# Linear attention and a mixture of four experts: k's last 64 rows multiplied as 64 partitions instead of zero-padded 128

## The chip, the core and the metric

The kernel runs on one core of a Trainium2 chip. The metric is the device time of one execution in microseconds (us), lower is better. The engines are named as the profile names them: PE is TensorE's matmul and PEld its weight load, DVE is VectorE, ACT is ScalarE, POOL is GpSimd and SP is SyncE, which only issues transfers here.

## What is computed

The reference is linear attention followed by four experts whose outputs are merged by the given probabilities:

```python
phi(x) = where(x > 0, x, exp(x) - 1) + 1        # q, k, v: (8, 8, 576, 64)
kv  = einsum('bhsd,bhse->bhde', phi(k), v)
z   = sum(phi(k), axis=2)
num = einsum('bhsd,bhde->bhse', phi(q), kv)
den = einsum('bhsd,bhd->bhs', phi(q), z) + 1e-6
x   = (num / den), as (4608, 512)
out = sum over e of p[:, e] * (relu(x @ w1[e]) @ w2[e])   # w1: (4, 512, 1024)
```

There are 8 batches of 8 heads, 576 rows to a head and 64 numbers to a row. The sum over the 576 rows in `kv` is where the change lies.

## The kernel before, in words

A head's 576 rows are four chunks of 128 and a rest of 64. The chunks go through the batch one after the other; the rests are kept apart. One tile, `rl`, holds the rests of k, v and q of a batch: partitions 0 to 63 have the 64 rest rows of heads 0 to 3, partitions 64 to 127 those of heads 4 to 7 (`load_left`, line 248).

**Phi.** It is computed as min(exp(x), max(x + 1, 1)) and written as f16. For the chunks `phi_act` and `phi_dve` (lines 303 and 318) write it. For the rests `left_act` and `left_dve` (lines 337 and 363) do. In batches 1 to 7 ScalarE writes x + 1 (line 351) and the exponential (line 355), the latter to PSUM, and VectorE joins them in one operation (line 367). In batch 0 ScalarE writes the exponential alone, and VectorE does two operations (lines 371 and 372). For q's rests each of these is one operation over 128 partitions. For k's rests the exponential is one operation, and each of the others is two, of 64 partitions, for they go to different columns of a tile with zeros: `kz` is 128 partitions x 4 pairs of heads x 128, and each pair has its phi in only one half of the partitions (the upper for heads 0 to 3, the lower for 4 to 7). The rest stays at the zero that line 134 writes once, at the start.

**Products of k and v.** `kv` (line 418) makes, for a pair of heads, one accumulation of five matmuls with 130 columns: four for the chunks (line 425) and one for the rest (line 432). Of the latter `kz[:, pair]` is the stationary operand with all 128 partitions, and the moving operand is `vl[:, 2a : 2a+2]`, which has the rests of v of two pairs, one in each half of the partitions. The zeros of `kz` take the wrong half out. The columns are 64 numbers for each of two heads, and for each a constant column that gives z. ScalarE then copies the two useful blocks to `kvz` (line 441). With 8 batches and 4 pairs there are 32 matmuls on line 432, between 128 on line 425. Numerators and denominators follow from `kvz` (`nd`, line 455; `nd_left`, line 478), and then x transposed.

**Experts.** Each of 9 token tiles (one of each batch, and one of all the rests) goes through the 4 experts. Layer 1 is made of seven products of half-size blocks, layer 2 of seven more (lines 730 and 668), with block sums of the hidden values on POOL (lines 635 to 641), relu on ACT and DVE (lines 714, 756 and 774) and the weighted sum of the outputs on DVE (line 570). The first tile with the first expert is done plainly (lines 524 and 579).

**Order.** The order of every engine's queue is written out by hand: a schedule is held fixed for PE, ACT, DVE, SP and POOL. Batch 0 follows the list `START`, in which a number stands for so many warming matmuls on a tile of zeros (line 857); `lka` and `lkd` are the phi of k's rests. The rest is a list of steps with positions that is sorted (`put_at`, line 919, and `work.sort`, line 992); `batch_steps` (line 799) places batch b + 1's attention among the experts of tile b, by the positions in `ATTN`. There `lk`, `lkd` and `kv` place ScalarE's part of k's rests, VectorE's part, and the products. The positions are the same before and after.

Weights come in through POOL's queue and most inputs through SP's. For batch 0, k's rests are the first transfer on SP.

Of the kernel before, what the change touches and what calls it, by code (L numbers as in the profile page):

```python
# [11 lines left out]
FP16 = mybir.dt.float16  # L12
# [18 lines left out]
            k=(-2.05, 25.8, 28.0, 28.5),  # L31
# [19 lines left out]
            k=(0.3, 2.9, 6.7, 11.25),  # L51
# [29 lines left out]
def kernel(  # L81
# [10 lines left out]
    nc = tc.nc  # L92
    ATTN, HSUM, L2ORD, L2AT, MODE = (CFG[x] for x in ("ATTN", "HSUM", "L2ORD", "L2AT", "MODE"))

    B, H, S, D = q.shape
# [3 lines left out]
    P = 128  # L99
    HP = P // 2  # L100
# [4 lines left out]
    HG = H // 2  # L105
    NPAIR = H // 2
# [17 lines left out]
    pconst = ctx.enter_context(tc.tile_pool(name="pconst", bufs=1))  # L124
# [5 lines left out]
    nc.gpsimd.memset(vl[:, :, D:DE], 1.0 / SX)  # L130
    qz = pconst.tile([P, 2, 2, P], FP16, tag="qz", name="qz")
    nc.vector.memset(qz, 0.0)
    kz = pconst.tile([P, NPAIR, P], FP16, tag="kz", name="kz")
    nc.vector.memset(kz, 0.0)
    kvzs = []
    for i in range(2):
        kvz = pconst.tile([P, NPAIR, 2, DE], FP16, tag=f"kvz{i}", name=f"kvz{i}")
# [31 lines left out]
    def aps(shape, dtype, name):  # L169
        return bank("aps", shape, dtype, name)  # L170
# [67 lines left out]
    class Batch:  # L238
        def __init__(self, b):
            self.b = b  # L240
            self.raw, self.ph, self.pairs = {}, {}, {}
            self.kvz, self.kl, self.qTl = kvzs[min(b, 1)], kz, qz
            self.ps = b >= 1

        def alloc_left(self):
# [91 lines left out]
        def left_act(self, *names):  # L337

            for name in names:
                i = ("k", "v", "q").index(name)  # L340
                src = self.rl[:, i].rearrange("p h d -> p (h d)")
                parts = []
                for u in range(2) if name == "k" else ():
                    us = slice(u * HP, (u + 1) * HP)
                    parts.append((us, self.kl[us, 2 * u : 2 * u + 2].rearrange("p a d -> p (a d)")))
                if name == "q":
                    self.ql = pa.tile([P, HG, D], FP16, tag="qlp", bufs=1, name="qlp")
                    parts.append((slice(0, P), self.ql.rearrange("p h d -> p (h d)")))
                if self.ps:
                    for us, dst in parts:  # L350
                        nc.scalar.activation(dst, src[us], AF.Identity, bias=1.0)
                    el = aps([P, HG * D], FP32, "psum_el")
                else:
                    el = pm.tile([P, HG * D], FP16, tag="hs0", bufs=2, name="el")
                nc.scalar.activation(el, src, AF.Exp)
                self.ph["l" + name] = src, el, parts
# [61 lines left out]
        def kv(self, pair0, n=2):  # L418
            ps = aps([P, 2, 2, DE], FP32, "psum_kv")
            for i in range(n):  # L420
                pair = pair0 + i
                hs = slice(2 * pair, 2 * pair + 2)
                a = pair % 2
                for c in range(CM):
                    nc.tensor.matmul(  # L425
                        out=ps[:, i],
                        lhsT=self.kp[:, c, hs],
                        rhs=self.vp[:, c, hs],
                        start=(c == 0),
                        stop=False,  # L430
                    )
                nc.tensor.matmul(
                    out=ps[:, i],
                    lhsT=self.kl[:, pair],
                    rhs=self.vl[:, 2 * a : 2 * a + 2],
                    start=False,
                    stop=True,
                )
            for u in range(2):
                us = slice(u * HP, (u + 1) * HP)  # L440
                nc.scalar.copy(
                    out=self.kvz[us, pair0 : pair0 + n, u, :], in_=ps[us, 0:n, u, :]
                )
# [419 lines left out]
    with tc.manual_schedule(  # L863
# [87 lines left out]
        for n, (j, e) in enumerate(units):  # L951
            h, hss = [None, None], [[None] * 4, [None] * 4]
# [72 lines left out]
```

## Time and profile before

| | |
|---|---|
| three runs | 497.23, 496.58, 497.17 us; median 497.17 |
| profiled execution | 497.03 us; its span from the first to the last instruction is 495.2 us |
| mean granted PE clock | 0.997 |
| instructions | 11600 in all; PE 4346 matmuls and as many loads, DVE 802, ACT 678, POOL 339 |
| line 432 (rest of k by rest of v) | 32 matmuls, 10.1 to 345.5 us |
| line 351 on k's rests | 14 operations of 413 ns on ACT |
| line 367 on k's rests | 14 operations of 414 ns on DVE |
| lines 371 and 372 on k's rests | 2 operations each, 460 and 645 ns, 284 and 289 ns, on DVE |
| zeros of `kz`, line 134 | 1 operation of 272 ns at 1.1 us on DVE |

A group's line in the profile has the source line, the engine, the operation, what it writes from what it reads, the partitions and elements, and how often. For a matmul the two numbers with a star are rows and columns of the array that it uses, and what follows is the result's shape. A matmul's end is modelled and lies after the start of the next one, so that starts are the better guide to what TensorE does. The products of batches 0 to 7 lie near 10 to 17, 55, 88, 139, 190, 242, 293 and 345 us.

### The profile page before, as it was taken

How to read it: one execution, taken by the hardware profiler on the slowest of the kernel's cores; microseconds unless marked ns; L12 is line 12 of the kernel's file. 1: busy time of each engine (PE TensorE's matmuls, PEld its weight loads, DVE VectorE, ACT ScalarE, POOL GpSimd, SP SyncE). 2: the span in 40 equal slices, each digit the busy share in tenths (PEclk: the TensorE clock that was granted, in tenths of full speed). 3: DMA queues.
4: the chain of work that ended last, by engine and by line, in shares of the span. 5: the costliest groups of instructions: out<-in, count | busy, mean ns of one | idle time of the engine just before them, and what ended most of it. 6: DMA issues, size and time to landing. Idle time of an engine off the chain costs nothing.

```text
span 495.2 us, 11600 instructions
## 1 busy us (share of the span) xinstructions
PE 482.3 (97%) x4346; PEld 409.1 (83%) x4346; DVE 379.0 (77%) x802; ACT 336.5 (68%) x678; POOL 354.6 (72%) x339
## 2 busy tenths in 40 slices
PE   8999989999999999999999999999999999999995
PEld 3556656888898989898989898989898888888884
DVE  6657988798967887698859886888687756775685
ACT  6766969964987498848884789468954565446530
POOL 3635204778967897769776977697769877987773
PEclk9999999999999999999999999999999999999998
DMA  8999965542455235533454245523231020002002
GB/s 257 213 220 241 271 136 176 165 112 52 110 188 114 57 109 174 124 63 102 141 152 77 77 144 141 99 63 104 71 76 28 5 95 1 1 8 80 1 1 86
DMA packets 81560, 53.65 MB, mean 108 GB/s; under 512 B 46112, under 2 KB 74784, under 8 KB 81504
## 3 DMA queue, kind: packets, MB, share of 16 engines
q1 hardware_dynamic: 70272, 40.07, 30.9%
q0 software_dynamic: 9824, 11.27, 12.1%
q10 hardware_dynamic: 1408, 1.57, 1.1%
q8 instruction: 34, 0.56, 0.5%
q14 instruction: 22, 0.18, 0.1%
HBM read 45.16 MB, written 9.44 MB: 110 GB/s over the span
## 4 chain that ended last, share of the span: by engine, by line
PE 79%; DMA 10%; ACT 5%; DVE 3%; issue 1%; POOL 1%; ACTq 0%; DVEq 0%; POOLq 0%
PE py L668 38%; PE pb L730 21%; PE pe L730 16%; DMA w<-in_moe_w_dram 7%; DMA rawu<-in_q_dram 2%; PE psum_nd L465 1%; DMA rawh<-in_k_dram 1%; PE psum_kv L425 1%; DVE acc L570 1%; ACT psum_ee L315 1%; DVE x_sb L448 1%; PE pb L668 1%; ACT u L741 1%; ACT vp L332 0%; ACT qp L310 0%
## 5 line engine op out<-in xcount | busy, mean ns | idle before, releaser
L570 DVE SCALAR_TENSOR_TENSOR acc<-py,p_sb,acc 128x256 f32<-128x256 f32 (+1 forms) x382 | 182.4, 488 | 49.1 <-PE py L668 39.9
L714 DVE CUSTOM_DVE_ANT_0 h<-pe,u 128x512 f16<-128x512 f32 x140 | 96.3, 688 | 41.8 <-PE pe L730 26.8
L730 PEld LDWEIGHTS <-w 128*128 128x128 f16 x1120 | 108.8, 98 | 17.0 <-issue 1.8
L635 POOL TENSOR_TENSOR hs<-h 128x512 f16<-128x512 f16 x64 | 74.0, 1156 | 54.9 <-DVE h L714 53.5
L668 PEld LDWEIGHTS <-h 128*128 128x128 f16 x1024 | 99.6, 98 | 11.8 <-issue 0.5
L668 PE MATMUL py<-w,h 128*128 128x256 f16 x744 | 106.3, 273 | 0.0
L741 ACT COPY u<-pb 128x512 f32<-128x512 f32 x140 | 82.8, 591 | 27.5 <-PE pb L730 25.3
L637 POOL TENSOR_TENSOR hs<-hs,h 128x512 f16<-128x512 f16 x64 | 74.7, 1167 | 26.7 <-PE py L668 24.1
L730 PEld LDWEIGHTS <-s 128*128 128x128 f16 x840 | 81.6, 98 | 11.7 <-DVE s L607 0.6
L730 PE MATMUL pb<-tt,w 128*128 128x256 f16 x560 | 84.0, 273 | 0.8 <-ACT u L741 0.7
L668 PEld LDWEIGHTS <-hs 128*128 128x128 f16 x768 | 74.4, 98 | 9.9 <-issue 1.3
L641 POOL TENSOR_TENSOR hs<-h,hs 128x512 f16<-128x512 f16 x64 | 74.6, 1165 | 3.5 <-PE py L668 3.0
L668 PE MATMUL py<-t,hs 128*128 128x256 f16 x496 | 74.4, 272 | 0.6 <-DVE acc L570 0.4
L639 POOL TENSOR_TENSOR h<-h 128x512 f16<-128x512 f16 x64 | 74.5, 1164 | 0.0
L756 ACT ACTIVATE h<-pe 128x512 f16<-128x512 f32 x70 | 41.9, 598 | 44.9 <-PE pe L730 44.4
L750 ACT COPY pe<-pb 128x512 f32<-128x512 f32 x70 | 40.2, 575 | 41.5 <-PE pb L730 14.9
L774 ACT ACTIVATE h<-pb 128x512 f16<-128x512 f32 x70 | 41.9, 599 | 10.1 <-PE pb L730 10.0
L730 PE MATMUL pb<-tt,s 128*128 128x256 f16 x280 | 42.0, 273 | 0.3 <-DVE s L607 0.3
L730 PE MATMUL pe<-tt,s 128*128 128x256 f16 x280 | 42.0, 273 | 0.0
L730 PE MATMUL pb<-xT,w 128*128 128x256 f16 x248 | 37.2, 273 | 0.1
L730 PE MATMUL pe<-xT,s 128*128 128x256 f16 x248 | 37.2, 273 | 0.0
L730 PE MATMUL pe<-xT,w 128*128 128x256 f16 x248 | 37.2, 273 | 0.0
(120 smaller groups left out, 604.4 us busy)
## 6 DMA issues: line engine op xcount, KB each, us to landing
out_dram<-acc SPq DMA_DIRECT2D x32, 256.0 KB, 2.5
w<-in_moe_w_dram POOLq DMA_DIRECT2D x14, 512.0 KB, 12.9
rawb<-in_v_dram SPq DMA_DIRECT2D x26, 256.0 KB, 2.8
rawb<-in_q_dram SPq DMA_DIRECT2D x26, 256.0 KB, 2.8
rawb<-in_k_dram SPq DMA_DIRECT2D x26, 256.0 KB, 3.2
w<-in_moe_w_dram POOLq DMA_DIRECT2D x4, 256.0 KB, 5.8
rawb<-in_k_dram POOLq DMA_DIRECT2D x4, 256.0 KB, 11.0
rl<-in_q_dram SPq DMA_DIRECT2D x16, 64.0 KB, 2.5
```

The lines of the kernel that those rows point to most:

```text
L570: nc.vector.scalar_tensor_tensor(out=acc, in0=ps, scalar=pscal, in1=acc, op0=AO.mult, op1=AO.add)
L635: nc.gpsimd.tensor_tensor(out=hs[0], in0=a21, in1=a22, op=AO.add)
L637: nc.gpsimd.tensor_tensor(out=hs[1], in0=hs[0], in1=a11, op=AO.subtract)
L639: nc.gpsimd.tensor_tensor(out=a21, in0=a11, in1=a21, op=AO.subtract)
L641: nc.gpsimd.tensor_tensor(out=hs[3], in0=a12, in1=hs[1], op=AO.subtract)
L668: nc.tensor.matmul(out=ps, lhsT=lhsT(k), rhs=rhs[:, k], start=first and k == 0, stop=k == FH - 1, skip_group_check=True,)
L714: nc.vector._custom_dve(TENSOR_ADD_SAT, out=out, in0=ps, in1=u, s0=BIG, s1=0.0)
L730: nc.tensor.matmul(out=ps[:, kk], lhsT=lk(kc), rhs=rhs[:, kc], start=first and kk == 0 and kc == 0, stop=kc == 1, skip_group_check=True,)
L741: nc.scalar.copy(u, self.b)
L750: nc.scalar.copy(self.e5, self.b)
L756: nc.scalar.activation(self.h[:, :, 0, 0:NH], self.e5, AF.Relu)
L774: nc.scalar.activation(self.h[:, :, 1, 0:NH], self.b, AF.Relu)
```

## The change

`kz` with its zeros is gone. In its place `kn` has 128 partitions x 4 x 64: as in `rl`, the upper half of the partitions has heads 0 to 3 and the lower half heads 4 to 7, four heads side by side. Phi of k's rests then has one destination over all 128 partitions, so lines 351, 367, 371 and 372 are issued once where they were issued twice. The matmul of a pair's rest takes 64 partitions of `kn` and the same 64 of `vl`: partitions 0 to 63 for pairs 0 and 1, 64 to 127 for pairs 2 and 3. The memory for `kz` (1 KB in each partition) becomes 512 bytes. Nothing else is edited.

```diff
-    kz = pconst.tile([P, NPAIR, P], FP16, tag="kz", name="kz")
-    nc.vector.memset(kz, 0.0)
+    kn = pconst.tile([P, HG, D], FP16, tag="kn", name="kn")
...
-            self.kvz, self.kl, self.qTl = kvzs[min(b, 1)], kz, qz
+            self.kvz, self.kl, self.qTl = kvzs[min(b, 1)], kn, qz
...
-                for u in range(2) if name == "k" else ():
-                    us = slice(u * HP, (u + 1) * HP)
-                    parts.append((us, self.kl[us, 2 * u : 2 * u + 2].rearrange("p a d -> p (a d)")))
+                if name == "k":
+                    parts.append((slice(0, P), self.kl.rearrange("p h d -> p (h d)")))
...
+                us = slice(pair // 2 * HP, (pair // 2 + 1) * HP)
                 nc.tensor.matmul(
                     out=ps[:, i],
-                    lhsT=self.kl[:, pair],
-                    rhs=self.vl[:, 2 * a : 2 * a + 2],
+                    lhsT=self.kl[us, 2 * a : 2 * a + 2],
+                    rhs=self.vl[us, 2 * a : 2 * a + 2],
                     start=False,
                     stop=True,
                 )
```

## The prediction

> **What bounds the kernel now.** I read four views in this order: the page's busy shares, the windows by stage, the timeline of TensorE around one of the changed matmuls, and the chain of work that ended last. The page says which engine is nearly always busy: its first line gives busy time, share of the span and instructions of each engine, the second each engine's share of the chain.
>
> ```profile
> PE 482.3 (97%) x4346; PEld 409.1 (83%) x4346; DVE 379.0 (77%) x802; ACT 336.5 (68%) x678; POOL 354.6 (72%) x339
> ...
> PE 79%; DMA 10%; ACT 5%; DVE 3%; issue 1%; POOL 1%; ACTq 0%; DVEq 0%; POOLq 0%
> ```
>
> 97% is an average over stages, and a matmul's recorded duration covers its neighbour's, so the stages have to be looked at. The windows view gives, for each stretch, its length, then busy time and count of TensorE, its weight loads, VectorE, ScalarE and GpSimd, then clock, DMA share and GB/s.
>
> ```profile
> 40.00:62.00 22.00, 21.20 (x160) 14.36 (x159) 17.66 (x30) 18.88 (x40) 8.96 (x13) 1.00 1.17 260
> 62.00:80.00 18.00, 16.34 (x124) 10.01 (x122) 14.43 (x34) 13.80 (x30) 4.63 (x5) 1.00 0.57 118
> 80.00:93.00 13.00, 12.85 (x114) 9.87 (x112) 9.89 (x19) 12.83 (x29) 7.33 (x7) 1.00 0.73 232
> 93.00:105.00 12.00, 11.50 (x105) 9.92 (x103) 11.66 (x19) 11.22 (x27) 9.15 (x8) 1.00 0.56 138
> 105.00:150.00 45.00, 44.85 (x429) 40.15 (x428) 37.46 (x82) 31.92 (x65) 36.13 (x33) 1.00 0.39 107
> 150.00:300.00 150.00, 150.00 (x1434) 135.10 (x1433) 121.33 (x264) 111.55 (x229) 120.79 (x110) 1.00 0.45 115
> 300.00:350.00 50.00, 50.00 (x480) 45.04 (x478) 40.95 (x89) 37.08 (x77) 39.61 (x37) 1.00 0.41 93
> 350.00:487.00 137.00, 136.70 (x1263) 122.33 (x1261) 97.55 (x203) 72.19 (x137) 110.13 (x98) 1.00 0.11 31
> ```
>
> Up to 62 us the DMA engines are full (share over 1). From 73 to 93 us the chain of waits runs almost without a break over ScalarE, which is busy 12.83 of 13 us. From 105 to 487 us TensorE has no hole. That it is truly dense there, and not only recorded so, is read from starts in TensorE's timeline (columns: start, length, instruction, count):
>
> ```profile
> 137.54 0.60 PE L730 MATMUL pe<-xT,w 128*128 128x256 f16 x4
> 137.98 0.39 PE L425 MATMUL psum_kv<-vp,kp 128*128 128x130 f16 x4
> 138.21 0.22 PE L432 MATMUL psum_kv<-vl,kz 128*128 128x130 f16 x1
> 138.26 0.39 PE L425 MATMUL psum_kv<-vp,kp 128*128 128x130 f16 x4
> 138.49 0.22 PE L432 MATMUL psum_kv<-vl,kz 128*128 128x130 f16 x1
> 138.55 0.60 PE L730 MATMUL pb<-tt,w 128*128 128x256 f16 x4
> ```
>
> The reader is to see that ten matmuls of 130 columns take 138.55 - 137.98 = 0.57 us, 57 ns each, although each is recorded with 220 ns: 163 ns of a record lies under the next one. A 256-column matmul follows the last after 0.44 / 4 = 110 ns. So in this stage whatever lengthens TensorE's stream lengthens the kernel, one for one, and whatever shortens another engine is hidden.
>
> The changed instructions, from the view of the tile kz (minimum/median/maximum ns):
>
> ```profile
> L432 PE MATMUL psum_kv<-vl,kz x32: 220/220/220, 10.1 to 345.5; 128*128 128x130 f16 x32
> L351 ACT ACTIVATE kz<-rl x14: 405/413/439, 40.2 to 336.0; 64x256 f16<-64x256 f32 x14
> L367 DVE SCALAR_TENSOR_TENSOR kz<-kz,psum_el x14: 402/414/425, 41.9 to 338.1; 64x256 f16<-64x256 f16 x14
> ```
>
> and, for the form of 128 partitions, from the view of psum_el:
>
> ```profile
> L367 DVE SCALAR_TENSOR_TENSOR qlp<-qlp,psum_el x8: 404/410/422, 74.0 to 393.2; 128x256 f16<-128x256 f16 x8
> ```
>
> **What the Trainium skill says.** TensorEngine Tiling, section Key Properties, says that changing the tiling mode, as opposed to the tile within a mode, drains TensorE; its list of configurations has 128x128 and 64x128 as different ones. It gives no price. Every matmul of this trace is marked 128*128, so no row here shows such a change. TensorE: Matmul & The Clock Gate, Single matmul latency, puts what is beyond the streamed columns at 398 cycles, 166 ns; the trace's 220 - 57 = 163 ns agrees. The same page, LDWEIGHTS, says that a load's time follows the columns and not the rows: both forms have 128 columns, so the load itself should stay at the traced 98 ns. Its section on the array's architecture lets TensorE pull weight loads ahead of matmuls in flight; the trace agrees (the load of 87.23 us starts before the matmul ahead of it ends).
>
> **The change part by part.**
>
> Phi of k's rests, batches 1 to 7: one ScalarE Identity of 64 partitions less (413 ns) and one VectorE operation less (414 ns) for each batch. The remaining one covers 128 partitions; q's rests show that form on VectorE at 410 ns, and on ScalarE at 419 to 478, so it costs up to 50 ns more there. Seven times 0.41 is 2.9 us on each of two engines. For batches 3 to 7 this lies at 130 to 338 us, beside a dense TensorE, and is worth nothing: ScalarE is there waiting for TensorE (line 756 alone 44.4 us in total). Batch 1's, at 40 us, lies in the stage of the full DMA. Batch 2's two Identities, 0.88 us together at 81.26 us, stand in the unbroken ScalarE chain of 73 to 93 us: **-0.42 us** at most.
>
> Phi of batch 0 on VectorE: line 371 falls from two (0.46 and 0.65 us) to one, line 372 from two (0.28 and 0.29) to one, 0.93 us in all. The first product needs only the first half, at 9.66 us, and gets the whole at the same time, since the single operations take the place of the first ones. VectorE then has to wait for psum_nd, ready at about 11.16 us, where it now starts on it at 11.30. So 0.14 us is left, before a stage that waits for weights: 0. The memset of kz (272 ns at 1.14 us) goes; VectorE's first phi waits until 5.05 for its data, so 0.
>
> The 32 matmuls of line 432, with their loads: number, columns and the 57 ns of streaming stay. New are the changes of mode: each stands between matmuls of 128 rows, so it has one change before it and one after it, 64 in all. The price is not in the trace. **Bounds for one change:** below, 0, if the array needs no emptying (nothing in the edit makes a matmul shorter, so no gain); above, 163 ns for letting the matmul ahead end, and some 55 ns more if the next load can't go ahead and shows (a load starts 87.23, its matmul 87.28). I take **163 ns**, since "drains" says that the work in flight ends, and that is what a record has beyond its streaming; the load's price is kept for the range.
>
> By stage, 2 x 0.163 = 0.33 us for each matmul:
> - batches 3 to 7 (138 to 345 us): 20 x 0.33 = **+6.5 us**, TensorE dense, all on the path;
> - batch 2 (87 to 89 us): 4 x 0.33 = 1.3 us; TensorE idles 0.15 us in 80 to 93 and 0.5 us in 93 to 105, which takes in half: **+0.65**;
> - batches 0 and 1 (10 to 17, 54 to 56 us): 2.6 us beside warming matmuls that compute nothing, and ahead of the q load that lands at 61.6: 0, at worst 2.6.
>
> No wait is added; VectorE's and ScalarE's queues only lose entries, and no DMA is moved. Sum: 6.5 + 0.65 - 0.42 = +6.7 us on the profiled 495.2, 501.9. The three plain runs have a median of 497.17, 2.0 above the span, so **503.9 us**.
>
> **The rivals.**
> - **No price for the mode** (also: the narrow operand runs as the full array, and the profile still says 128*128). For it: the page gives no number, and the load is no longer. Against it: its plain sentence. Then only -0.42 us is left: 496.8. This is the case that ends on the other side, not slower; its mechanism is the ScalarE chain at 81 us, and it decides once a change of mode costs under 0.42 / 40 = 10 ns.
> - **Only the load shows.** The array needn't empty, but the next load isn't pulled ahead: 55 ns a change. 40 x 0.055 = 2.2, batch 2 0.2, less 0.42: +2.0, 499.2.
> - **Drain and load both show**, 218 ns a change: 40 x 0.218 = 8.7, batch 2 0.9, less 0.42: +9.2, 506.4.
> - **The shorter queues are worth more.** VectorE's 0.14 us at 11 us and ScalarE's 0.42 at 81 both pass on, and a buffer comes free sooner in the chain over VectorE and GpSimd at 101 to 107 us, where the chain leaves TensorE: at most another 0.5 us: 496.1. It needs a free change of mode too.
>
> **How the numbers follow.** Drain as priced 0.40, own range 503.3 (batch 2 hidden) to 505.0 (batch 2 in full, no ScalarE gain); drain and load, or the early batches showing too, 0.13; only the load 0.15; no price 0.26; worth more 0.06. A difference of 0.2%, 1 us, is about what can be told from no change. Faster by more: 0.07; within: 0.25 (the no-price case); slower: 0.68. Range 496.6 to 507.0: the low end takes in the no-price case, the high end the dearer drain; about 0.1 is left out on each side.
>
> **What would show it.** Line 432 would read 64*128. In the timeline at 138 us, the time from line 432's start to the next start would grow from 57 to about 220 ns, and likewise that before it; ten matmuls would take 1.2 instead of 0.57 us. If those starts are still 57 ns apart, the drain is wrong and so is the prediction. If they are 110 apart, only the load shows. ScalarE's chain should lose 0.4 us at 81 us in any case, and the phi groups should fall from 14 to 7. If TensorE's stream past 105 us is longer for another reason than line 432, the mechanism is wrong though the sign may be right.

## The result, and the profile after

The changed kernel is slower: 501.85 us median of four runs (501.25 to 501.91) against 496.88 for the kernel before (496.58 to 497.23). The ratio is 1.0094 with an interval of 1.0079 to 1.0109. The profiled execution is the fastest of the four, with a span of 499.4 us against 495.2.

On the page of the changed kernel, the busy shares and the chain:

```profile
PE 488.4 (98%) x4346; PEld 410.6 (82%) x4346; DVE 374.8 (75%) x792; ACT 334.2 (67%) x671; POOL 354.7 (71%) x339
...
PE 85%; DMA 9%; DVE 3%; POOL 2%; issue 1%; DVEq 0%; POOLq 0%
```

VectorE has 10 instructions less and ScalarE 7, as the edit says, and both are less busy. TensorE has exactly as many matmuls as before, and its recorded busy time is 6 us longer. ScalarE, 5% of the chain before, is gone from it.

The view of the tile kn shows the new forms (line 431 is the product that was line 432; 349 and 365 were 351 and 367):

```profile
L431 PE MATMUL psum_kv<-vl,kn x32: 227/228/228, 10.1 to 349.7; 64*128 64x130 f16 x32
L349 ACT ACTIVATE kn<-rl x7: 408/424/468, 39.9 to 339.0; 128x256 f16<-128x256 f32 x7
L365 DVE SCALAR_TENSOR_TENSOR kn<-kn,psum_el x7: 407/410/410, 41.6 to 341.1; 128x256 f16<-128x256 f16 x7
```

The recorded matmul went from 220 to 228 ns, which would be 0.26 us over all 32 and says nothing of the loss. It is in the starts. TensorE's timeline of the changed kernel, at the place that was shown of before:

```profile
137.65 0.60 PE L729 MATMUL pe<-xT,w 128*128 128x256 f16 x4
138.08 0.39 PE L423 MATMUL psum_kv<-vp,kp 128*128 128x130 f16 x4
138.40 0.23 PE L431 MATMUL psum_kv<-vl,kn 64*128 64x130 f16 x1
138.56 0.40 PE L423 MATMUL psum_kv<-vp,kp 128*128 128x130 f16 x4
138.90 0.23 PE L431 MATMUL psum_kv<-vl,kn 64*128 64x130 f16 x1
139.06 0.61 PE L729 MATMUL pb<-tt,w 128*128 128x256 f16 x4
```

Ten matmuls of 130 columns take 139.06 - 138.08 = 0.98 us, where they took 0.57. Four chunks take 0.32 to 0.34 us up to the rest (0.23 before), and a rest 0.16 us up to what follows (0.06 before). The difference of 0.41 us over four changes of mode is **0.103 us for one**. The weight loads stand differently too. Before, a rest's load starts some 55 ns ahead of its matmul, while the matmul ahead is still recorded as running; these two lines are of batch 2 in the kernel before:

```profile
87.23 0.10 PEld L432 LDWEIGHTS <-kz 128*128 128x128 f16 x1
87.28 0.22 PE L432 MATMUL psum_kv<-vl,kz 128*128 128x130 f16 x1
```

In the changed kernel the load starts together with its matmul:

```profile
138.40 0.09 PEld L431 LDWEIGHTS <-kn 64*128 64x128 f16 x1
```

The load of the wide matmul after a rest waits in the same way (both start at 138.56). The windows view of the changed kernel shows what the later starts do to a stage in which TensorE has no hole:

```profile
150.00:300.00 150.00, 150.00 (x1411) 133.34 (x1409) 118.61 (x259) 108.00 (x220) 118.25 (x108) 1.00 0.43 110
```

TensorE is as full as before, but gets through 1411 matmuls in 150 us instead of 1434. The clock granted is the same.

Where the 4.2 us between the two spans lie is read off the first product of a batch. A batch has two stretches of ten matmuls like the one shown, 2 x 0.41 = 0.82 us, and the distance from one batch's first product to the next one's, from 138 us on, is indeed 52.0 us instead of 51.2. Five batches (3 to 7) cost 5 x 0.82 = 4.1 us. Batch 3's first product starts at 138.08 instead of 137.98, so all that comes earlier, gains and losses together, makes 0.1 us.

### The profile page after: what moved, and what is told of

The parts are those of the page before. It is cut to its first block, busy times and chain, and to the rows that moved or that the text cites. A ratio compares the mean times of both kernels' runs of the same rounds, so it can differ in the third digit from the quotient of the medians.

```text
span 499.4 us, 11586 instructions
## 1 busy us (share of the span) xinstructions
PE 488.4 (98%) x4346; PEld 410.6 (82%) x4346; DVE 374.8 (75%) x792; ACT 334.2 (67%) x671; POOL 354.7 (71%) x339
## 4 chain that ended last, share of the span: by engine, by line
PE 85%; DMA 9%; DVE 3%; POOL 2%; issue 1%; DVEq 0%; POOLq 0%
PE py L667 37%; PE pb L729 23%; PE pe L729 17%; DMA w<-in_moe_w_dram 7%; PE py L578 3%; PE psum_kv L423 2%; PE psum_nd L464 1%; DMA rawb<-in_v_dram 1%; PE psum_kv L431 1%; DVE acc L569 1%; DMA rl<-in_k_dram 1%; POOL w L182 1%; DVE h L713 1%; PE pb L667 1%; DVE x_sb L447 1%
```

## The experiments

Three theories stood against each other: a price for each change of the array's mode, a price for each narrow matmul whatever its neighbours are, and a loss in the phi or the new tile. Two more runs (rests_four, rests_outer) then asked what the price depends on, and three (v_padded, v_padded_pool, before_pool) whether the saving on ScalarE and VectorE can be had without it. The timelines are of one execution of each kernel. Ratios are to the kernel before on the same chip.

**rows64_only: the narrow product alone.** The kernel before, with this edit, in which `us` is the pair's half of the partitions:

```diff
-                    lhsT=self.kl[:, pair],
-                    rhs=self.vl[:, 2 * a : 2 * a + 2],
+                    lhsT=self.kl[us, pair],
+                    rhs=self.vl[us, 2 * a : 2 * a + 2],
```

> Before, with one edit: line 432's product takes 64 partitions of kz and of vl instead of 128; kz keeps its zeros and phi of k's rests stays at two operations. Theory 1, each change of the array's mode costs 0.103 us (64 changes, 40 of them from 105 us on): the whole loss of the change and a bit more, since ScalarE's 0.4 us at 81 us is not saved: 501.4 to 502.8 us, ratio to before 1.009 to 1.012, and starts around line 432 as in the changed kernel (about 150 and 160 ns). Theory 2, each narrow matmul is slow in itself: the same time. Theory 3, the loss is in the phi or the new tile: no slower than before, 496.5 to 497.4.

Measured: 502.19 us, ratio 1.0095 (1.0082 to 1.0108). The product alone brings the whole loss; the third theory falls. It stays open here whether the mode or the narrow matmul is priced.

**phi_only: the phi alone.**

```diff
-                    lhsT=self.kl[us, 2 * a : 2 * a + 2],
-                    rhs=self.vl[us, 2 * a : 2 * a + 2],
+                    lhsT=self.kl[:, 2 * a : 2 * a + 2],
+                    rhs=self.vl[:, 2 * a : 2 * a + 2],
```

> The changed kernel with line 432's product over all 128 partitions of kn and vl, so each pair's sum also takes in the rests of the pair two further on; the phi is the one operation of the change. Theories 1 and 2: no 64-row matmul, so no loss is left, and the shorter ScalarE queue at 81 us brings 0 to 0.6 us: 496.3 to 496.9, ratio 0.9985 to 1.000. Theory 3: as slow as the changed kernel, 501 to 502.

Measured: 496.85 us against 497.53, ratio 0.9988 (0.9980 to 0.9996). No loss is left, and the shorter phi is worth 0.2 to 1.0 us. ScalarE's timelines show a part of it; first before, then phi_only, with the lines between left out:

```profile
79.80 0.58 ACT L750 COPY pe<-pb 128x512 f32<-128x512 f32 x1
...
81.26 0.88 ACT L351 ACTIVATE kz<-rl 64x256 f16<-64x256 f32 x2
...
83.85 0.63 ACT L310 ACTIVATE kp<-rawb 128x512 f16<-128x512 f32 x1
```

```profile
80.25 0.58 ACT L749 COPY pe<-pb 128x512 f32<-128x512 f32 x1
...
81.71 0.47 ACT L349 ACTIVATE kn<-rl 128x256 f16<-128x256 f32 x1
...
83.53 0.60 ACT L773 ACTIVATE h<-pb 128x512 f16<-128x512 f32 x1 [0.27 <-PE pb L729]
84.03 0.62 ACT L309 ACTIVATE kp<-rawb 128x512 f16<-128x512 f32 x1
```

One operation of 0.47 us stands where two took 0.88. From the copy to `kp` it is 3.78 us instead of 4.05: ScalarE gets 0.27 us ahead, and on the way it now waits 0.27 us for TensorE. From the copy to batch 2's first product it is 7.03 us instead of 7.26, so 0.23 us arrives there; the changed kernel has 7.03 too. After that nothing more of the phi shows: from batch 2's first product to batch 3's it is 50.93 us in both kernels, and from batch 3's to batch 7's 204.7 us in both. The product's price for batch 2 is read off the same distance: 51.62 us in rows64_only and 51.61 in the changed kernel, 0.69 more.

From batch 0's first product to batch 3's it is 128.07 us before and 127.70 in phi_only, 0.37 less. The part of this that lies ahead of the copy can't be put down to the phi: the way from batch 0's first product to batch 1's alone varies from 43.7 to 44.9 us among the profiles of the ten kernels.

**rests_adjacent: the same matmuls, fewer changes.** In the changed kernel the second pair of a call takes its rest first:

```diff
+                terms = [rest] + terms if i % 2 else terms + [rest]
```

> The changed kernel with the rest of every second pair first in its accumulation instead of last, so that in batches 1 to 7 the two rests of a call stand next to each other: the same matmuls, 36 changes of mode instead of 64, and from 105 us on 20 instead of 40. Theory 1 (price for a change of mode): 20 x 0.103 = 2.1 us less from 105 us on and up to 0.4 us in batch 2: 499.3 to 499.9 us, and the second rest starts 57 ns after the first. Theory 2 (price for a narrow matmul): unchanged, 501.4 to 502.1, and the second rest's start or what follows is as late as now.

Measured: 499.08 us, ratio 1.0037 (1.0025 to 1.0050), 0.57% below the changed kernel's ratio, 2.8 us. Its timeline:

```profile
137.41 0.39 PE L427 MATMUL psum_kv<-vp,kp 128*128 128x130 f16 x4
137.73 0.29 PE L427 MATMUL psum_kv<-vl,kn 64*128 64x130 f16 x2
137.95 0.40 PE L427 MATMUL psum_kv<-vp,kp 128*128 128x130 f16 x4
138.19 0.60 PE L721 MATMUL pb<-tt,w 128*128 128x256 f16 x4
```

The ten matmuls take 0.78 us, midway between 0.57 and 0.98. The record of the two rests is 0.29 us long and that of one 0.22 to 0.23, so the second starts some 60 to 70 ns after the first, close to the ordinary step of 57. A narrow matmul next to a narrow one costs at most some 10 ns extra; the second theory falls. From batch 4 on the distance from batch to batch is 51.60 us, again midway between 51.18 and 52.01.

The expectation of 499.3 to 499.9 was missed by 0.2 us on the low side, and the whole time is not made of the price alone. Batch 1 starts 43.72 us after batch 0 instead of 44.37 in the changed kernel, though the changes of mode between the two are as many in both; this is the stretch that varies so. Against that, TensorE waits 0.28 us for ScalarE at 149 us, so that from batch 3 to batch 4 nothing is gained (52.04 us).

**rests_four: all four rests of a batch together.** In batches 1 to 7 the products of both calls are made in one stretch, in this order:

```diff
+            chunks(0, True)
+            chunks(2, True)
+            rest(0, False)
+            rest(1, True)
+            rest(2, False)
+            rest(3, True)
+            chunks(1, False)
+            chunks(3, False)
```

> The changed kernel with the four rests of a batch in one stretch, in batches 1 to 7 (two in partitions 0 to 63, then two in 64 to 127; the first two products move to the place of the last two): 2 changes of mode for a batch instead of 8, from 105 us on 10 instead of 40. If a change of mode is priced and a change between the two halves within the mode is free: 3.1 us less than the changed kernel from 105 us on and some 0.6 in batch 2, ratio to before 1.001 to 1.003, and the third rest starts 57 to 70 ns after the second. If the change between the halves is priced like one of mode: 0.5 us more than that, and the third rest starts 150 ns after the second.

Measured: 498.40 us, ratio 1.0021 (1.0014 to 1.0029). The timeline:

```profile
141.19 0.62 PE L429 MATMUL psum_kv<-vp,kp 128*128 128x130 f16 x8
141.74 0.29 PE L440 MATMUL psum_kv<-vl,kn 64*128 64x130 f16 x4
141.97 0.63 PE L429 MATMUL psum_kv<-vp,kp 128*128 128x130 f16 x8
142.43 0.60 PE L776 MATMUL pe<-xT,s 128*128 128x256 f16 x4
```

Twenty matmuls take 1.24 us, where 20 x 57 ns would be 1.14: 0.10 more for two changes, less than the 0.21 of the price. Four rests take 0.23 us, hardly longer than two in rests_adjacent (0.22). The windows view of this kernel, for the instructions on kn alone, shows why, with that of rests_adjacent after it:

```profile
141.75:141.76 0.01, 0.01 (x2) 0.01 (x4) 0.00 (x0) 0.00 (x0) 1.00 0.00 0
...
141.80:141.82 0.02, 0.02 (x4) 0.02 (x4) 0.00 (x0) 0.00 (x0) 1.00 0.00 0
```

```profile
137.75:137.78 0.03, 0.03 (x1) 0.03 (x2) 0.00 (x0) 0.00 (x0) 1.00 0.97 341
```

The count after TensorE's busy time is the number of matmuls that touch the stretch. Within 20 ns of the first start two are under way, where in rests_adjacent there is one. So two steps of 57 ns are saved, and 2 x 0.103 - 2 x 0.057 = 0.09 us is what a batch should cost more than before; from 193.25 to 347.11 us three batches take 51.29 us each against 51.18. My expectation of 57 to 70 ns from the second rest to the third was wrong. The trace does not name the half of each start. Two rests of the same half start 60 to 70 ns apart in rests_adjacent, so the two that start together here are taken to be one of each half: the third in the program then begins ahead of the second, and the two halves run side by side.

The profiled execution is the slowest of this kernel's (499.66 us, against the median of 498.40). TensorE's longest wait in it after 105 us is 0.61 us for ScalarE (`acc`) at 151 us. Whether moving the first call causes it is not shown: shorter waits for the same operation, 0.17 to 0.28 us at 149 to 151 us, are in v_padded, rests_outer and rests_adjacent, whose calls stand where they stood.

**rests_outer: does the price depend on the matmul ahead?** The same edit as rests_adjacent with the two orders exchanged, so the number of changes is the changed kernel's.

> The changed kernel with the first rest of a call at its very start and the second at its very end: as many changes of mode as in the change, but one entry in two now comes after a matmul of 256 columns instead of 130. If a change adds a fixed time on top of the streaming of the matmul ahead: that rest starts 110 + 100 = 210 ns after the start of the last 256-column matmul, and the time is the changed kernel's, 501.4 to 502.6, ratio 1.008 to 1.011. If it is a floor between two starts of about 150 ns: 150 ns there, 20 entries or exits of 50 ns less, about 1 us faster than the changed kernel, ratio 1.006 to 1.008.

Measured: 501.85 us, ratio 1.0091 (1.0074 to 1.0108).

```profile
138.12 0.60 PE L721 MATMUL pe<-xT,w 128*128 128x256 f16 x4
138.65 0.23 PE L427 MATMUL psum_kv<-vl,kn 64*128 64x130 f16 x1
138.81 0.63 PE L427 MATMUL psum_kv<-vp,kp 128*128 128x130 f16 x8
```

Four matmuls of 256 columns take 0.53 us up to the narrow one, and 0.44 up to a wide one: 0.09 on top, as after 130 columns. The entry is an addition, not a floor of 150 ns between two starts. Every return to wide matmuls follows a narrow one of 130 columns in all these runs, so for the way out this stays untested.

**v_padded, v_padded_pool and before_pool: the saving without the price.** In v_padded the zeros lie around v's rests, so that the product takes 128 partitions and the phi is one operation; the copy of v's rests becomes two. In v_padded_pool, and in before_pool with nothing else changed, batch 2's copies of v's rests go to GpSimd. The edits against the kernel before, without the lines that make the tile and its copies; v_padded has those above the dots, before_pool those below, v_padded_pool both:

```diff
-                    lhsT=self.kl[:, pair],
-                    rhs=self.vl[:, 2 * a : 2 * a + 2],
+                    lhsT=self.kl[:, 2 * a : 2 * a + 2],
+                    rhs=self.vl[:, pair],
...
-        put(at["lv"], bt.left_v)
+        put(at["lv"], bt.left_v, *((nc.gpsimd,) if bt.b == 2 else ()))
```

> The zeros are moved from k's rests to v's: kn and its one phi operation as in the change, and vl with a block for each pair and zeros in the other half's partitions, so the product has 128 partitions. The copy of v's rests becomes two of 64 partitions; VectorE loses one operation for each batch, ScalarE one Identity and gains one copy. Theory 1 and 2: no change of mode, VectorE's saving hidden: 496.5 to 497.3, ratio 0.999 to 1.001. If VectorE's queue were worth something on the path: under 496.4.

> v_padded (zeros in v's rests, phi of k's rests one operation, no change of mode) with batch 2's two copies of v's rests on GpSimd, so that ScalarE loses 0.85 us at 82 us in its unbroken stretch of 73 to 93 us. If that stretch sets when the dense stage begins: 0.4 to 0.9 us faster than before, ratio 0.998 to 0.9993. If TensorE, dense from 86 us, sets it: ratio 0.9993 to 1.0005.

> Before with one edit: batch 2's copy of v's rests on GpSimd instead of ScalarE, which loses 0.40 us at 83 us, about what the change's shorter phi takes from it there. If ScalarE's stretch sets the start of the dense stage: 0.2 to 0.5 us faster, ratio 0.999 to 0.9996, much as phi_only; otherwise 0.9996 to 1.0004.

Measured: ratios 0.9999 (0.9990 to 1.0008), 0.9993 (0.9983 to 1.0002) and 0.9994 (0.9985 to 1.0004). VectorE's saving without ScalarE's, in v_padded, is worth nothing that can be seen in the time. The two others lean to the fast side by 0.3 us, but their intervals take in no change. No version that computes the reference is shown to beat the kernel before.

The traces say what became of ScalarE's relief. In before_pool and in v_padded_pool it is 3.78 us from the copy to `kp`, the same 0.27 us ahead as in phi_only, though v_padded_pool takes 0.85 us from ScalarE: the rest turns into waiting for TensorE (0.56 us). In before_pool TensorE then loses the 0.27 us again:

```profile
85.41 0.39 PE L482 MATMUL psum_nl<-kvz,qz 128*128 128x130 f16 x4 [0.30 <-DVE kp L322]
```

It waits for VectorE, which there still has two phi operations of k's rests, 0.84 us together. From the copy to batch 2's first product it is 7.26 us in before_pool, as before; 7.19 in v_padded, where VectorE alone is relieved; and 7.03 in phi_only and v_padded_pool, where both are. In these single profiles the gain in batch 2 takes both shorter queues.

## Why the prediction was right, and which size was off

- **TensorE's stream decides from 105 us on: right.** Between 105 and 487 us it idles only 0.15 us near 107 us and 0.3 us after 350 us, in both kernels, and the loss is there: 4.1 of the 4.2 us of the spans.
- **A change of mode is priced: right, and shown.** rows64_only has the whole loss; rests_adjacent halves it for each batch from batch 4 on, with the same matmuls. The rivals without a price fell with the first of these. The sentence of the Trainium skill, TensorEngine Tiling, Key Properties, that changing the mode, and not just the tile, drains TensorE agrees with what the runs show: 0.103 us for a change of mode, and no more than some 10 ns between narrow matmuls. That the array is emptied is not itself seen in a trace.
- **The size of one change: off, and it is the term that made the sum too large.** I took 163 ns, all that a matmul's record has beyond its streaming. It measured 103, between my bounds of 0 and 218. The record's modelled end isn't what the next load waits for: in the changed kernel the chunks that start at 138.08 us are recorded to 138.47, and the rest's load starts at 138.40. For batches 3 to 7 the measured price makes 40 x 0.103 = 4.1 us instead of the 6.5 of the sum; in all, 6.7 us was forecast and 5.0 measured in the medians. The rival in which only the load shows, at 55 ns, is 48 ns too low where the 163 is 60 too high.
- **Batch 2: the number right, in part by luck.** The sum had 0.65 us, half of 1.3. From batch 2's first product to batch 3's, 0.69 us shows. But its four products at the measured price come to 0.82 us, so that 0.13 us was hidden, and not half: a price too high and too much hiding came out even. Batches 0 and 1, put at nothing, can't be told from what varies there.
- **ScalarE's saving at 81 us: the right place, a smaller size.** At most 0.42 us was forecast. ScalarE gets 0.27 us ahead, then waits for TensorE, and 0.23 us reaches batch 2's first product. In batch 2 VectorE's saving, put at nothing, is a condition of it: before_pool, with ScalarE's relief alone, has no gain there. Alone, VectorE's saving brings nothing that can be told in the time (v_padded).
- **The weight load.** Its recorded time went from 98 to 93 ns, and did not grow with half the rows. It no longer starts ahead of its matmul, as the rivals with the load had it. How much of the 103 ns is the array emptying, and how much the load that could not go ahead, no run separates.

With the measured price, batches 3 to 7 make 4.1 us, and all that comes before, from batch 0's first product to batch 3's, 128.31 - 128.07 = 0.24 us: 4.3 us, beside 4.2 in the spans and 5.0 in the medians.

## What to carry to other kernels

Zeros that fill a matmul up to the full array can be cheaper than leaving them out. Here the step from one matmul to the next follows the columns (57 ns for 130, 110 for 256) and a narrow product's step was no shorter, while each switch between 128 and 64 rows cost TensorE about 0.1 us on the way in and again on the way out. Where such products are wanted, put them next to each other, so that a stretch pays twice and not each product. And when TensorE is dense, weigh any saving on another engine by the one stage in which that engine is the bound: here some 0.2 of 2.9 us, and that only where the next engine in the chain was relieved too.

## What was not expected of the hardware

- A change of mode adds about 0.1 us to the start of the next matmul: on the way in 0.09 to 0.10, after 130 columns and after 256 alike, and on the way out 0.10, after 130 columns. The matmul's own record grew by only 8 ns.
- Products on partitions 0 to 63 and on 64 to 127 that stand in one stretch seem to run side by side without being asked to: four took 0.23 us where two in the same half took 0.22. Which half each start belongs to is inferred, as said at rests_four.
